# Transposing q and k with DMAs instead of TensorE in the later blocks of a linear-attention and SiLU-MLP kernel

## The chip, the core and the metric

The kernel runs on one core of a Trainium2 chip. The core has five engines that work side by side: TensorE for matrix products (PE in the profile; PEld is its loading of weights), VectorE (DVE), ScalarE (ACT), GpSimd (POOL) and SyncE (SP), which here issues DMAs. Each engine takes its instructions in the order in which the program lists them, and semaphores make one wait for another. Sixteen DMA engines move data between HBM and SBUF, the on-chip memory; PE writes into eight banks of PSUM. The metric is the device time of one execution in microseconds, as the median of several.

## The reference

There are 4 sequences of 768 positions, with 8 heads of 64 elements. Attention is linear with decay: each head h has a factor lam, and

```python
for b in range(nb):
    intra = np.einsum('bhic,bhjc->bhij', qb, kb) * Dmask[None]
    intra = np.einsum('bhij,bhjd->bhid', intra, vb)
    inter = np.einsum('bhid,bhde->bhie', qb * lam_pow[None], kv_state)
    out[:, :, sl] = intra + inter
    kb_dec = kb * rev_pow[None]
    kv_state = lam_block * kv_state + np.einsum('bhsd,bhse->bhde', kb_dec, vb)
```

Dmask is lower triangular with powers of lam. The 3072 rows of 512 that come out go through two dense products with a SiLU between them:

```python
h = x @ w_in                      # 512 -> 2048
g = h * (1.0 / (1.0 + np.exp(-h)))
return g @ w_out                  # 2048 -> 512
```

Inputs and output are float32; the kernel's products take bf16 operands.

## The kernel before

**Attention by blocks.** The 3072 rows are cut into 24 blocks of 128 positions, 6 to a sequence. For a block u the kernel loads k and v (128 positions by 8 heads by 64, float32, 256 KB each) with one DMA each (line 261). q is loaded for two blocks at once (line 264, 512 KB) except for blocks 0, 1, 22 and 23, which are called plain. DVE scales q by powers of lam into bf16 `qs` (line 315) and k into bf16 `ks` (line 369). Scores need q and k with the head's elements on the partitions, so both are transposed. In the kernel before, PE does this with an identity matrix into a PSUM bank: four 128x128 transposes for each block of q (line 327), four for each block of k (line 389). From there ACT or DVE copies q into `qT` (line 336) and k into `kTz` (line 397). In `kTz` each head of a pair of heads stands on its 64 partitions and the other 64 hold zeros, so that a product with the pair's `qT` yields the scores of one head alone. Spreading keys so takes two copies of 64 partitions by 512 elements. For the first 8 blocks (`WIDE = 8`) the zeros are put in before the transpose: `ks` is a padded tile `kp` (line 361), there are eight transposes (line 377) and one copy of 1024 elements, and the state's product is done by head (line 480, eight products of 64 columns) and not by pair of heads (line 484, four of 128), with one sum on DVE (line 500) and not two halves.

Then PE computes scores (line 415), DVE applies the mask and evicts them as `st_sb` (line 424), PE multiplies them with the values `vz` and adds the state's part (lines 453 and 457), and ACT or DVE evicts the result as `xt`. The state is carried from block to block by the sum on line 500 and two multiplications on POOL.

**The dense part.** Attention rows are grouped (first groups of 1 or 2 blocks, later of 4). For a group the first product (line 545) takes 13.8 us of PE when it has 4 blocks; SiLU runs on ACT (line 554); the second product (line 573) runs block by block, then an eviction and a store. The weights are loaded and cast between the first loads of attention.

**The order of the work.** Nothing is emitted in the order of the loops. Every step is handed to a planner (`Plan`, lines 14 to 96) with the engines that may do it and an assumed duration on each, the steps it needs, a priority, and the buffers that it takes and frees (`alloc`, `frees`, named rings with a fixed number of slots). `Plan.run` simulates this greedily and emits all instructions by planned start time. So each engine's order is fixed when the program is written, by assumed durations. Loads form one chain on a resource "SP": 1.19 us for a k, 1.15 for a v, 1.8 for a q of two blocks, 1.36 for a weight piece; they are emitted `AHEAD = 1.8` us before their planned start. A step of resource "NONE" takes no time and can carry a delay: from block 8 on, q, k and v are held to be there only 4.0 us after their load's end (`late`, lines 307 and 355). Stores are a resource "STORE", but are issued from SP too, so loads and stores share one queue in order of planned time. PE idle time before 90 us of the plan may be filled with warm-up products (line 650).

The names that matter below: `kf`, `vf`, `qf` are the rings of loaded blocks (6, 6 and 3 slots), `qs` (2), `qT` (4), `ks` (4), `kTz` (3) those of scaled and transposed blocks, `tr` a PSUM bank for transposes (two at a time).

Of the kernel before, what the change touches and what calls it, by code (L numbers as in the profile page):

```python
# [8 lines left out]
BF16 = mybir.dt.bfloat16  # L9
# [4 lines left out]
class Plan:  # L14
# [3 lines left out]

    AHEAD = 1.8
    AWAY = 0.6  # L20
    LAT = {"SP": 0.0, "NONE": 0.0, "STORE": 2.0, "PE": 0.25, "DVE": 0.12, "ACT": 0.16, "POOL": 0.15, "DMA": 0.1}

    def __init__(self):
        self.ops = []
# [75 lines left out]
def kernel(  # L100
# [10 lines left out]
    nc = tc.nc  # L111
    B, H, S, D = q.shape
    assert (B, H, S, D) == (4, 8, 768, 64)
    BLK = 128
    NB = S // BLK
    NU = B * NB
    NP = H // 2
# [3 lines left out]
    KI = DM // 128  # L121
    KO = DFF // 128
    HB = BLK // 2
    WIDE = 8

    ctx.enter_context(tc.manual_schedule())
    const = ctx.enter_context(tc.tile_pool(name="const", bufs=1))
# [1 line left out]
    ps = ctx.enter_context(tc.tile_pool(name="ps", bufs=1, space=bass.MemoryType.PSUM))  # L129

    plan = Plan()
    BUFS = dict(kf=6, vf=6, qf=3, wst=6, qs=2, qT=4, ks=4, g=34, st_sb=6, o_sb=3, y=2, Xf=2,
                kTz=3, vz=3, Xz=2, kp=3)
    for name, n in BUFS.items():
        plan.ring(name, n)
    plan.ring("bank", 8, pick=True)
# [4 lines left out]
    def sb(o, name, shape, dtype, tag=None):  # L141
        return work.tile(shape, dtype, tag=tag or name, bufs=BUFS[tag or name], name=name)

    def bank(o, name, shape, dtype):
# [5 lines left out]
        out=lam_sb,  # L150
        in_=bass.AP(tensor=lam.tensor, offset=lam.offset, ap=[[0, 128]] + list(lam.ap)),
# [17 lines left out]
        out=ident, in_=ident, compare_op=AL.not_equal, fill=1.0,  # L169
# [6 lines left out]
        out=mask, in_=mask, compare_op=AL.is_ge, fill=0.0,  # L176
        base=0, pattern=[[1, BLK]], channel_multiplier=-1,
    )

    kTz = [const.tile([128, NP, 2, BLK], BF16, name=f"kTz{i}") for i in range(BUFS["kTz"])]  # L180
    vz = [const.tile([128, NP, 4, 64], BF16, name=f"vz{i}") for i in range(BUFS["vz"])]
    Xz = [const.tile([128, NP, 128], BF16, name=f"Xz{i}") for i in range(BUFS["Xz"])]
    kp = [const.tile([128, NP, 2, 128], BF16, name=f"kp{i}") for i in range(BUFS["kp"])]
# [19 lines left out]
    for hh in range(2):  # L203
        r = slice(64 * hh, 64 * hh + 64)
# [15 lines left out]
    val = {}  # L220

    def copy(o, dst, src):
        if o["eng"] == "ACT":
            nc.scalar.activation(dst, src, AF.Copy)  # L224
        else:
            (nc.vector if o["eng"] == "DVE" else nc.gpsimd).tensor_copy(dst, src)  # L226
# [20 lines left out]
    for n, (kind, j) in enumerate(order):  # L247
# [7 lines left out]
        def fn(o, kind=kind, j=j, tag=tag):  # L255
            b, blk = divmod(j, NB)
            sl = slice(blk * BLK, (blk + 1) * BLK)
            if kind in "kvq" and tag != "qf":
                t = sb(o, kind + "f", [128, H, 64], F32, tag)
                src = dict(k=k, v=v, q=q)[kind]  # L260
                nc.sync.dma_start(out=t, in_=src[b, :, sl, :].rearrange("h s d -> s h d"))
            elif kind == "q":
                t = sb(o, "qf", [128, H, 128], F32)
                nc.sync.dma_start(
                    out=t, in_=q[b, :, blk * BLK:(blk + 2) * BLK, :].rearrange("h (p t) d -> p h (t d)", t=2))
            elif kind == "i":
                t = sb(o, "wst", [128, 2, 512], F32)
                m, a = divmod(j, 2)
                nc.sync.dma_start(out=t, in_=w_in_r[:, 2 * a:2 * a + 2, m * 512:(m + 1) * 512])
            else:  # L270
                t = sb(o, "wst", [128, 2, DM], F32)
                nc.sync.dma_start(out=t, in_=w_out_r[:, 2 * j:2 * j + 2, :])
            val[kind + "f", j] = t


        o = plan.op({"SP": us}, [prev], fn, n, alloc=[tag])
# [18 lines left out]
    O = {}  # L295

    def attention(u):
        b, blk = divmod(u, NB)
        pr = at["v", u]


        if u in plain or u % 2 == 0:
            two = u not in plain
            lq = load["q", u]
            late = []
            if u >= 8:
                late = [plan.op({"NONE": 0.0}, [lq], lambda o: None, 0, after=4.0)]
            halves = []
            for t in range(2 if two else 1):
                def fn(o, t=t, first=(t == 0)):  # L310
                    qf = val["qf", u]
                    if first:
                        val["qs", u] = sb(o, "qs", [128, 2, H, 64], BF16)
                    src = qf.rearrange("p h (t d) -> p h t d", t=2)[:, :, t, :] if two else qf
                    nc.vector.tensor_tensor(  # L315
                        val["qs", u][:, t], src,
                        lam_fwd[:, 1 + t if two else 0, :, None].to_broadcast([128, H, 64]), op=AL.mult)
                halves.append(plan.op(
                    {"DVE": 0.7}, [lq] + late + halves[:1], fn, pr + 0.1, alloc=["qs"] if t == 0 else [],
                    frees=[(lq, lq["tag"])] if t == two else []))  # L320
            trs = []
            for t in range(len(halves)):
                def fn(o, t=t):
                    if t == 0:
                        val["trq", u] = bank(o, "tr", [128, len(halves), NP, BLK], BF16)
                    for i in range(NP):
                        nc.tensor.transpose(val["trq", u][:, t, i, :], val["qs", u][:, t, 2 * i:2 * i + 2, :], ident)  # L327
                trs.append(plan.op({"PE": 0.225}, [halves[t]] + trs[:1], fn, pr + 0.1,
                                   alloc=["bank", "n_tr"] if t == 0 else [],
                                   frees=[(halves[0], "qs")] if t == len(halves) - 1 else []))  # L330
            evs = []
            for t in range(len(halves)):
                def fn(o, t=t):
                    if t == 0:
                        val["qT", u] = sb(o, "qT", [128, 2, NP, BLK], BF16)
                    copy(o, val["qT", u][:, t], val["trq", u][:, t])
                evs.append(plan.op({"ACT": 0.6, "DVE": 0.69}, [trs[t]] + evs[:1], fn, pr + 0.1,
                                   alloc=["qT"] if t == 0 else [],
                                   frees=[(trs[0], "bank"), (trs[0], "n_tr")] if t == len(halves) - 1 else []))
            O["qT", u] = evs  # L340
            if two:
                O["qT", u + 1] = evs
        home = u if u in plain else u - u % 2

        def qT(p):
# [5 lines left out]

        lk, lv = load["k", u], load["v", u]
        late = []
        if u >= 8:
            late = [plan.op({"NONE": 0.0}, [lv], lambda o: None, 0, after=4.0)]

        wide = u < WIDE
        if wide:
# [13 lines left out]
        ks = plan.op({"DVE": 0.7}, [lk] + late, fn, pr, alloc=[ring_k], frees=[(lk, lk["tag"])])  # L372
        if wide:
            def fn(o):
                val["trk", u] = bank(o, "tr", [128, 2 * NP, BLK], BF16)
                for i in range(2 * NP):
                    nc.tensor.transpose(val["trk", u][:, i, :], val["ks", u][:, i // 2, i % 2, :], ident)  # L377
            tk = plan.op({"PE": 0.45}, [ks], fn, pr, alloc=["bank", "n_tr"])

            def fn(o):  # L380
                val["kTz", u] = kTz[o["slots"]["kTz"]]
                copy(o, val["kTz", u].rearrange("p a b s -> p (a b) s"), val["trk", u])
            kz = [plan.op({"ACT": 1.02, "DVE": 1.22}, [tk], fn, pr, alloc=["kTz"],
                          frees=[(tk, "bank"), (tk, "n_tr")])]
        else:
            def fn(o):
                val["trk", u] = bank(o, "tr", [128, NP, BLK], BF16)
                for i in range(NP):
                    nc.tensor.transpose(val["trk", u][:, i, :], val["ks", u][:, 2 * i:2 * i + 2, :], ident)  # L389
            tk = plan.op({"PE": 0.225}, [ks], fn, pr, alloc=["bank", "n_tr"])  # L390
            kz = []
            for hh in range(2):
                def fn(o, hh=hh):
                    if hh == 0:
                        val["kTz", u] = kTz[o["slots"]["kTz"]]
                    r = slice(64 * hh, 64 * hh + 64)
                    copy(o, val["kTz", u][r, :, hh, :], val["trk", u][r])
                kz.append(plan.op({"ACT": 0.59, "DVE": 0.69}, [tk] + kz[:1], fn, pr,
                                  alloc=["kTz"] if hh == 0 else [],
                                  frees=[(tk, "bank"), (tk, "n_tr")] if hh else []))  # L400
# [9 lines left out]
        for half in range(2):  # L410
            def fn(o, half=half):
                val["st", u, half] = bank(o, "st", [128, 4, BLK], F32)
                for i in range(4):
# [5 lines left out]
                         alloc=["bank", "n_st"])  # L419

            def fn(o, half=half):
# [6 lines left out]
                                 frees=[(st, "bank"), (st, "n_st")]))  # L428
# [16 lines left out]
        def fn(o):  # L445
# [4 lines left out]
            for p in range(NP):  # L450
# [5 lines left out]
                if blk > 0:  # L456
                    nc.tensor.matmul(x[:, p, :], lhsT=val["Xz", u][:, p, :], rhs=qT(p), start=False, stop=True)  # L457
        oo = plan.op({"PE": 0.0556 * (8 if blk == 0 else 12)}, masks + [vc] + prev_x + ([O["out", u - 1]] if u else []), fn, pr + 0.4,
                     alloc=["bank", "n_x"], frees=gives)
# [14 lines left out]
        def fn(o):  # L474
            d = bank(o, "d", [128, NP, 64 if wide else 128], F32)
            val["d", u] = d
            for p in range(NP):
# [5 lines left out]
                else:  # L483
# [4 lines left out]
                     alloc=["bank", "n_d"], frees=[(ks, ring_k)])  # L488
# [161 lines left out]
                nc.tensor.matmul(t, lhsT=zeros[:, 0:128], rhs=zeros, start=True, stop=True)  # L650
        seq.append((a, len(seq), dict(fn=fn)))

    seq = plan.run({"PE": 1.9, "DVE": 4.2, "ACT": 5.9, "POOL": 5.0, "SP": 3.7, "STORE": 0.0, "NONE": 0.0}, idle)
    for _, _, o in seq:
        o["fn"](o)

# [29 lines left out]
```

## Time and profile before

Three runs took 235.18, 235.65 and 235.69 us, a median of 235.65. The profiled execution is another one:

| | |
|---|---|
| profiled execution, whole | 237.28 us |
| its span, first to last instruction | 235.6 us |
| busy: PE / DVE / ACT / POOL | 221.8 / 114.7 / 121.9 / 53.1 us |
| mean granted TensorE clock | 0.998 |
| moved by DMA | 33.85 MB in 73060 packets, 55376 of them under 512 B |
| landing of a k, v, double q load after issue (median) | 5.5, 5.3, 5.9 us |
| last load issued | 109.34 us |
| last dense product ends | 230.5 us |

How to read the views: a group's row names line, engine, operation, written tile, read tiles, shape and count; then busy time, mean nanoseconds of one, and the idle time of the engine just before, with what ended it. In a timeline the columns are start, length and the instruction, with the wait before it in brackets. The rows of stretches give busy time of each engine within a window. The chain of waits goes back from the last instruction to what released each step. Matmuls are pipelined, so the mean of one is longer than the time from one to the next; the chain shows the latter.

### The profile page before, as it was taken

To read this page: it belongs to the slowest core of one execution; us is meant where nothing else is said; L and a number is where in the kernel's file an instruction comes from. 1 tells how busy PE (TensorE), PEld (TensorE's weight loads), DVE (VectorE), ACT (ScalarE), POOL (GpSimd) and SP (SyncE) were. 2 spreads that over 40 slices of the span, in tenths; PEclk is the share of its full clock that TensorE was granted. 3 is DMA by queue.
4 is the path that set the end of the run, shared out by engine and by line. 5 is a ranking of instruction groups with operands and counts; after the bars stand their busy time and mean duration, and the time that the engine had idled before them with its cause. 6 is when DMAs were issued, how large, how long until landed. Compare 5 with 4: busy or idle time off the path is not lost.

```text
span 235.6 us, 4440 instructions
## 1 busy us (share of the span) xinstructions
PE 221.8 (94%) x1799; PEld 136.3 (58%) x1799; DVE 114.7 (49%) x184; ACT 121.9 (52%) x213; POOL 53.1 (23%) x71
## 2 busy tenths in 40 slices
PE   4889898999999999979999999999999999999994
PEld 1656687899756676746667544444444444444453
DVE  5677755694359999998997211012100111021221
ACT  5585477867777699869976422401275023710000
POOL 7354420340045244642476100000000000000000
PEclk9999999999999999999999999999999999999999
DMA  6999989999999999999200122204400232023232
GB/s 124 237 288 298 294 227 226 296 363 318 221 228 245 255 262 222 233 238 219 46 1 12 35 47 45 45 2 87 92 0 0 45 75 61 0 45 83 56 86 89
DMA packets 73060, 33.85 MB, mean 144 GB/s; under 512 B 55376, under 2 KB 66000, under 8 KB 73040
## 3 DMA queue, kind: packets, MB, share of 16 engines
q1 hardware_dynamic: 72896, 33.50, 60.4%
q8 instruction: 14, 0.23, 0.4%
q10 hardware_dynamic: 144, 0.07, 0.1%
q14 instruction: 6, 0.05, 0.1%
HBM read 27.27 MB, written 6.29 MB: 142 GB/s over the span
## 4 chain that ended last, share of the span: by engine, by line
PE 52%; DVE 2%; DMA 1%; ACT 1%; issue 0%; DVEq 0%
PE o_ps L573 28%; PE h_ps L545 19%; PE x_ps L453 1%; PE st_ps L415 1%; DVE st_sb L424 1%; PE o_ps L612 1%; DMA out_dram<-o_sb 1%; PE x_ps L457 1%; PE d_ps L484 1%; PE tr_ps L327 0%; PE tr_ps L389 0%; DVE ks L369 0%; DVE y L500 0%; ACT kTz L224 0%; DVE o_sb L226 0%
## 5 line engine op out<-in xcount | busy, mean ns | idle before, releaser
L545 PE MATMUL h_ps<-xt,w_in_bf 128*128 128x512 bf16 (+2 forms) x576 | 88.9, 308 | 0.0
L554 ACT ACTIVATE g<-h_ps 128x512 bf16<-128x512 f32 x96 | 56.3, 597 | 59.2 <-PE h_ps L545 33.0
L573 PE MATMUL o_ps<-w_out_bf,g 128*128 128x512 bf16 x368 | 83.3, 379 | 0.5 <-DVE st_sb L424 0.5
L545 PEld LDWEIGHTS <-w_in_bf 128*128 128x128 bf16 x576 | 49.7, 98 | 29.1 <-DVE w_in_bf L226 0.3
L226 DVE COPY o_sb<-o_ps 128x512 f32<-128x512 f32 (+2 forms) x24 | 15.9, 663 | 87.1 <-PE o_ps L573 84.5
L573 PEld LDWEIGHTS <-g 128*128 128x128 bf16 x368 | 35.2, 98 | 39.6 <-issue 0.7
L229 POOL TENSOR_TENSOR Xz<-y,lam_blk 64x256 bf16<-64x256 f32 x40 | 34.3, 858 | 75.0 <-DVE y L500 46.0
L424 DVE TENSOR_TENSOR st_sb<-st_ps,mask 128x512 bf16<-128x512 f32 x48 | 30.9, 683 | 6.0 <-PE st_ps L415 5.7
L224 ACT ACTIVATE kTz<-tr_ps 64x512 bf16<-64x512 bf16 (+1 forms) x38 | 25.8, 680 | 6.6 <-PE tr_ps L377 2.2
L315 DVE TENSOR_TENSOR qs<-qf,lam_fwd 128x512 bf16<-128x512 f32 x24 | 20.2, 861 | 5.0 <-DMA qf<-in_q_dram 5.0
L224 ACT ACTIVATE xt<-x_ps 128x512 bf16<-128x512 f32 x24 | 14.2, 594 | 9.2 <-PE x_ps L457 8.8
L453 PE MATMUL x_ps<-st_sb,vz 128*128 128x128 bf16 x192 | 18.0, 219 | 0.2
L453 PEld LDWEIGHTS <-vz 128*128 128x128 bf16 x192 | 15.1, 98 | 5.4 <-issue 1.2
L500 DVE TENSOR_TENSOR y<-d_ps,Xf 64x256 f32<-64x256 f32 (+1 forms) x27 | 11.3, 419 | 9.9 <-issue 7.6
L415 PE MATMUL st_ps<-qT,kTz 128*128 128x128 bf16 x192 | 15.1, 222 | 0.5 <-ACT qT L224 0.3
L224 ACT ACTIVATE qT<-tr_ps 128x512 bf16<-128x512 bf16 x22 | 12.8, 594 | 4.4 <-PE tr_ps L327 4.3
L229 POOL TENSOR_TENSOR Xf<-y,lam_blk 128x256 f32<-128x256 f32 x16 | 14.5, 909 | 1.3
L457 PE MATMUL x_ps<-qT,Xz 128*128 128x128 bf16 x80 | 14.5, 219 | 0.0
L415 PEld LDWEIGHTS <-kTz 128*128 128x128 bf16 x192 | 12.5, 99 | 3.1 <-ACT kTz L224 1.0
L224 ACT ACTIVATE o_sb<-o_ps 128x512 f32<-128x512 f32 (+1 forms) x2 | 0.9, 438 | 25.6 <-DMA out_dram<-o_sb 25.6
L369 DVE TENSOR_TENSOR ks<-kf,lam_bwd 128x512 bf16<-128x512 f32 x16 | 14.0, 879 | 0.3
L327 PE MATMUL tr_ps<-ident,qs 128*128 128x128 bf16 x96 | 9.1, 223 | 4.0 <-DVE qs L315 3.8
(54 smaller groups left out, 115.8 us busy)
## 6 DMA issues: line engine op xcount, KB each, us to landing
kf<-in_k_dram SPq DMA_DIRECT2D x24, 256.0 KB, 5.5
vf<-in_v_dram SPq DMA_DIRECT2D x24, 256.0 KB, 5.3
out_dram<-o_sb SPq DMA_DIRECT2D x41, 128.0 KB, 2.4
qf<-in_q_dram SPq DMA_DIRECT2D x10, 512.0 KB, 5.9
wst<-in_moe_w_in_dram SPq DMA_DIRECT2D x8, 512.0 KB, 6.9
wst<-in_moe_w_out_dram SPq DMA_DIRECT2D x8, 512.0 KB, 7.3
qf<-in_q_dram SPq DMA_DIRECT2D x4, 256.0 KB, 5.1
out_dram<-o_sb SPq DMA_DIRECT2D x3, 256.0 KB, 3.6
```

The costliest lines, as they stand in the source:

```text
L224: nc.scalar.activation(dst, src, AF.Copy)
L226: (nc.vector if o["eng"] == "DVE" else nc.gpsimd).tensor_copy(dst, src)
L229: (nc.vector if o["eng"] == "DVE" else nc.gpsimd).tensor_tensor(dst, a, b, op=op)
L315: nc.vector.tensor_tensor(val["qs", u][:, t], src, lam_fwd[:, 1 + t if two else 0, :, None].to_broadcast([128, H, 64]), op=AL.mult)
L369: nc.vector.tensor_tensor(val["ks", u], val["kf", u], lam_bwd[:, :, None].to_broadcast([128, H, 64]), op=AL.mult)
L415: nc.tensor.matmul(val["st", u, half][:, i, :], lhsT=val["kTz", u][:, h // 2, h % 2, :], rhs=qT(h // 2), start=True, stop=True)
L424: nc.vector.tensor_tensor(val["st_sb", u, half], val["st", u, half], m[:, None, :].to_broadcast([128, 4, BLK]), op=AL.mult)
L453: nc.tensor.matmul(x[:, p, :], lhsT=vp[:, p, hh, :], rhs=val["st_sb", u, h // 4][:, h % 4, :], start=(hh == 0), stop=(hh == 1 and blk == 0))
L457: nc.tensor.matmul(x[:, p, :], lhsT=val["Xz", u][:, p, :], rhs=qT(p), start=False, stop=True)
L545: nc.tensor.matmul(t[:, j, :], lhsT=w_in_bf[:, ko, (m * per + j) * 128:(m * per + j + 1) * 128], rhs=xts[g][:, ko, :], start=(ko == 0), st ...
L554: nc.scalar.activation(t, val["h", g, m], AF.Silu)
L573: nc.tensor.matmul(val["o", u], lhsT=val["g", g, ko][:, i * BLK:(i + 1) * BLK], rhs=w_out_bf[:, ko, :], start=(ko == 0), stop=(ko == KO - 1))
```

## The change

From block `XB = 8` on, PE transposes neither q nor k. SP issues a transposing DMA from SBUF to SBUF in their place: for q, `qs` goes to `qT` in one DMA for both blocks of a pair (one for a plain block); for k, `ks` goes to a new tile `kT` (ring of 3), from which two copies of 64 partitions spread the keys into `kTz` as before, now reading SBUF, with DVE named first. The planner is given a new resource "XBAR" for these DMAs, one after another, at 2.0 us for 128x512 elements (4.0 for a pair's q), and what needs them is planned 3.0 us after that. They are issued on SP, in the same queue as loads and stores, without the 1.8 us that loads are emitted ahead. The copies and banks of the q transposes disappear for these blocks.

For blocks 4 to 7 the loads of q, k and v are now counted 1.2 us late. Padded keys are used for four blocks in place of eight, so blocks 4 to 7 go by the narrow path, still with transposes on PE. The `qf` ring has 2 slots in place of 3.

```diff
-    LAT = {"SP": 0.0, "NONE": 0.0, "STORE": 2.0, ...
+    LAT = {"SP": 0.0, "XBAR": 0.0, "NONE": 0.0, "STORE": 2.0, ...
...
-    WIDE = 8
+    XB = 8
+    WIDE = 4
...
-    BUFS = dict(kf=6, vf=6, qf=3, wst=6, qs=2, qT=4, ks=4, g=34, st_sb=6, o_sb=3, y=2, Xf=2,
-                kTz=3, vz=3, Xz=2, kp=3)
+    BUFS = dict(kf=6, vf=6, qf=2, wst=6, qs=2, qT=4, ks=4, g=34, st_sb=6, o_sb=3, y=2, Xf=2,
+                kTz=3, vz=3, Xz=2, kp=3, kT=3)
...
-            if u >= 8:
-                late = [plan.op({"NONE": 0.0}, [lq], lambda o: None, 0, after=4.0)]
+            if u >= 4:
+                late = [plan.op({"NONE": 0.0}, [lq], lambda o: None, 0, after=4.0 if u >= 8 else 1.2)]
...
+            if u >= XB:
+                n = len(halves)
+
+                def fn(o):
+                    val["qT", u] = sb(o, "qT", [128, 2, NP, BLK], BF16)
+                    nc.sync.dma_start_transpose(
+                        out=val["qT", u][:, 0:n].rearrange("p t a s -> p (t a) s"),
+                        in_=val["qs", u][:, 0:n].rearrange("p t h d -> p (t h d)"))
+                x = plan.op({"XBAR": 2.0 * n}, [halves[-1]], fn, pr + 0.1, alloc=["qT"], frees=[(halves[0], "qs")])
+                O["qT", u] = [x, plan.op({"NONE": 0.0}, [x], lambda o: None, 0, after=3.0)]
-            for t in range(len(halves)):
+            for t in range(len(halves) if u < XB else 0):
...
-        if u >= 8:
-            late = [plan.op({"NONE": 0.0}, [lv], lambda o: None, 0, after=4.0)]
+        if u >= 4:
+            late = [plan.op({"NONE": 0.0}, [lv], lambda o: None, 0, after=4.0 if u >= 8 else 1.2)]
...
+        elif u >= XB:
+            def fn(o):
+                val["kT", u] = sb(o, "kT", [128, NP, BLK], BF16)
+                nc.sync.dma_start_transpose(
+                    out=val["kT", u], in_=val["ks", u].rearrange("p h d -> p (h d)"))
+            tk = plan.op({"XBAR": 2.0}, [ks], fn, pr, alloc=["kT"])
+            landed = plan.op({"NONE": 0.0}, [tk], lambda o: None, 0, after=3.0)
+            kz = []
+            for hh in range(2):
+                def fn(o, hh=hh):
+                    if hh == 0:
+                        val["kTz", u] = kTz[o["slots"]["kTz"]]
+                    r = slice(64 * hh, 64 * hh + 64)
+                    copy(o, val["kTz", u][r, :, hh, :], val["kT", u][r])
+                kz.append(plan.op({"DVE": 0.35, "ACT": 0.59}, [tk, landed] + kz[:1], fn, pr,
+                                  alloc=["kTz"] if hh == 0 else [], frees=[(tk, "kT")] if hh else []))
...
-    seq = plan.run({"PE": 1.9, ..., "SP": 3.7, "STORE": 0.0, "NONE": 0.0}, idle)
+    seq = plan.run({"PE": 1.9, ..., "SP": 3.7, "STORE": 0.0, "NONE": 0.0, "XBAR": 0.0}, idle)
```

## The prediction

> **What bounds the kernel now.** I read the share of busy time first, then the busy time by stage, because an average hides that three resources take turns.
>
> ```profile
> PE 221.8 (94%) x1799; PEld 136.3 (58%) x1799; DVE 114.7 (49%) x184; ACT 121.9 (52%) x213; POOL 53.1 (23%) x71
> PEclk9999999999999999999999999999999999999999
> ```
> ```profile
> 70.00:80.00 10.00, 9.70 (x98) 6.33 (x96) 9.78 (x17) 7.22 (x13) 5.15 (x6) 1.00 1.03 259
> 80.00:90.00 10.00, 10.00 (x114) 7.16 (x112) 9.76 (x17) 8.96 (x17) 3.01 (x4) 1.00 1.11 241
> 90.00:100.00 10.00, 10.00 (x107) 6.93 (x106) 9.78 (x16) 9.00 (x17) 5.96 (x7) 1.00 0.98 235
> 100.00:110.00 10.00, 8.61 (x85) 5.64 (x84) 9.87 (x16) 7.84 (x15) 4.14 (x5) 1.00 1.27 232
> 110.00:120.00 10.00, 10.00 (x104) 6.89 (x103) 9.04 (x15) 9.32 (x19) 4.88 (x6) 1.00 0.39 68
> ```
> The columns after the length are PE, PEld, DVE, ACT and POOL busy time, the granted clock, the DMA share and GB/s. From 70 to 110 us PE is full, DVE is full (39.2 of 40 us), and the DMA engines are full. After 115 us nothing is loaded any more, and from 120.7 us on the chain of waits is PE alone, from 133.8 us dense products only, to 230.5 us. The clock never falls. So PE work taken out anywhere after about 50 us shortens the span, if PE isn't made to wait: its order is fixed when the program is written, and an operand that comes later than the planner thought stops everything behind it. It hardly happens now. The waits from 60 us on are 0.30, 1.39 and 0.46 us.
>
> ```profile
> 103.45 0.40 PE L484 MATMUL d_ps<-vz,ks 128*128 128x128 bf16 x4 [1.39 <-DVE vz L226]
> 120.73 1.02 PE L573 MATMUL o_ps<-w_out_bf,g 128*128 128x512 bf16 x4 [0.46 <-DVE st_sb L424]
> ```
> The third view is the load queue, SP's timeline.
>
> ```profile
> 59.80 1.13 SPq L264 DMA_DIRECT2D qf<-in_q_dram  x1
> ...
> 103.34 1.09 SPq L261 DMA_DIRECT2D qf<-in_q_dram  x1
> 104.53 1.04 SPq L261 DMA_DIRECT2D kf<-in_k_dram  x1
> 105.66 1.23 SPq L261 DMA_DIRECT2D vf<-in_v_dram  x1
> 106.94 1.14 SPq L261 DMA_DIRECT2D qf<-in_q_dram  x1
> 108.13 1.11 SPq L261 DMA_DIRECT2D kf<-in_k_dram  x1
> 109.34 1.09 SPq L261 DMA_DIRECT2D vf<-in_v_dram  x1
> ```
> The reader is to see that SP issues load after load without a pause, each held about 1.1 us by the full queue (an issue into an emptier one took 0.42 us). Six pairs of blocks lie between the two q rows: 43.54 / 6 = 7.26 us a pair. The planner counts 1.80 + 2 x 1.19 + 2 x 1.15 = 6.48 us a pair, so the loads slip 0.78 us a pair, some 5 us over the stage, and PE paid 2.15 us of it in waits, a share of 0.43. The rest went into the 4 us by which blocks from 8 on are counted late.
>
> **The sum's base.** Span 235.6 us; the profiled execution took 237.28 us in all, so 1.7 us lie around the span. The median of the runs shown, 235.65, is 1.6 us under that execution. I add the terms to the span and read the result as a median: both are 235.6.
>
> **PE: transposes leave.** Two rows carry it (groups by form).
>
> ```profile
> L389 PE MATMUL tr_ps<-ident,ks 128*128 128x128 bf16 x64 | 6.0, 219 | 0.0
> L327 PE MATMUL tr_ps<-ident,qs 128*128 128x128 bf16 x64 | 5.7, 219 | 0.4 <-DVE qs L315 0.3
> ```
> They are of the stretch from 60 to 135 us: count, busy us, mean ns of one, idle before. The 64 on line 327 are 7 pairs at 8 and 2 single blocks at 4, so this is exactly what blocks 8 to 23 need, and all 128 go. The mean of 219 ns overlaps with its neighbours; in the chain of waits four take 0.22 us and eight 0.45, 55.6 ns each: 128 x 0.0556 = 7.1 us. All lie in the stage where PE is the limit: **-7.1 us**, hidden by nothing.
>
> **Blocks 4 to 7.** Unpadded keys halve 32 transposes (16 x 0.0556 = 0.9 us) and turn 24 products of line 480 (1.2 us) into 12 of 0.0556 (0.7 us): 1.4 us of PE. Counting the loads 1.2 us late moves dense work in front of operations that PE waited for at 40.71 (1.00 us) and 47.39 (0.75 us). At best -3.2; at worst the three more halved sums on DVE (3 x 0.42 us) come onto the path, +1.3. Work saved before 50 us partly becomes waiting: I take the middle of the better half, **-1.5**.
>
> **ACT and DVE.** ACT loses 30 key copies (17.6 us) and 15 query copies (8.6 us). DVE gains 32 copies of 64x512; the nearest row, the same shape from PSUM, took 0.413 us, so 13.2 us less the three PSUM copies it loses (1.2): 12 us on an engine that has 0.8 us free between 70 and 110. The cover is ACT: it has 26 us less, and casts of values, evictions of outputs and of attention results can go there. Value **0**; without that cover up to +6 (half of 12, the other half lying in 110 to 130, where DVE has 3 us free in 20); below nothing -2, the ACT relief answering the 1.39 and 0.46 us waits.
>
> **SP and the DMA engines.** 16 transposing DMAs for k, 7 for q pairs, 2 for the q of the last blocks: 25 issues, 32 units of 128x512 bf16 (131 kB). All stand in SP's queue, between the loads, and share its rings. No row shows one. Lower end by bytes: 131 kB at the best slice of the page, 363 GB/s: 0.36 us. Upper end: the 2.0 us a unit that the planner is given for them; a store of the same size, 128 KB, took 2.4 us from issue to landing, alone. I take a price by packets: a k load is 1024 packets of 256 B at 1.1 us, a unit of bf16 rows cut into 128 columns has 512 of the same size, so 0.55 us. How many get in front of the last load? The planner runs them one after another at 2.0 us from the first keys (60.1 us, first line 369) to the last load (109.3): at most 24; the q pairs wait for their second half, so 21. The last load then issues 21 x 0.55 = 11.5 us later, at about 121 us.
>
> [...]
>
> What part of 11.5 us reaches PE? Between the measured share of 0.43 (4.9 us) and all of it. I take all: the 4 us of lateness are used up by today's slip, and the transposing DMA itself stands in SP's order behind the slipping loads, then has scores (line 415) on PE and masks on DVE queued behind it. **+11.5**. The qf ring of two costs nothing: the q load at 89.45 needs the buffer that the scaling at 83.52 frees, 4.6 us earlier; without that, its wait would be a load's 1.1 us.
>
> **New waits.** SP now waits for the scaled block (line 369 or 315) before it issues a transposing DMA, with later loads and stores behind it. Today's loads land 5.3 to 5.9 us after issue; the planner allows 2.0 + 3.0. **+0.5**; at the ends 0, and 1 us at each of 17 issues before the last load, +17.
>
> **Sum**: -7.1 - 1.5 + 0 + 11.5 + 0.5 = +3.4, so 239.0 us (profiled execution about 240.7).
>
> **Rivals.** *Slip absorbed, faster.* Speaking for it: 5 us of slip cost PE 2.15. At 0.36 us a unit, 7.6 x 0.43 = 3.3: -8.6 + 3.3 + 0.5 gives 230.8; with nothing charged, 227.0. Against: no margin is left in the load queue. It decides below a delay of 8.1 us, which is 0.39 us a unit if all of it is paid. Chance 0.37.
> *Transposing DMAs much dearer, or SP held at each wait, slower by far.* 1.0 us a unit gives 21 us, 248.5; 2.0 gives 42, 269.5; SP waits of 1 us add 17, 255.5. For it: full rings, in-order SP. Against: loads in flight keep the rings fed for about 5 us while SP waits. Chance 0.17.
> *Change not felt*: the two sides cancel within 0.2% (0.5 us), about what a measurement of this kernel can tell from no change. Chance 0.04.
> *Forecast*, 236.2 to 247: 0.42.
>
> **Numbers.** Slower 0.42 + 0.17 = 0.59, faster 0.37, same 0.04. The range goes from 229 (under it the case with next to nothing charged, 0.09) to 254 (above it 0.11). The likeliest case alone spans 236.2 to 247.
>
> **What will show it.** No tr_ps groups after block 8, and about 1.4 us less of them and of line 480 before; the last load issued near 121 us (109 or less speaks for the first rival, 130 or more for the second); PE waits between 70 and 130 us of about 12 us, released by kTz, qT or st_sb; landing of the transposing DMAs at 5 to 6 us. The prediction is wrong if the DMA share has room that the page doesn't show, if the planner's 2.0 us a unit spreads attention so that slipping loads meet no waiting PE, or if DVE's copies, not SP, hold the scores.

## The result and the profile after

The changed kernel takes 242.91 us (median of four, 241.59 to 244.82) against 235.48 us: a ratio of 1.031, with a 95% interval of 1.025 to 1.037. It is slower by 7.4 us. The forecast was 3.4 us, the right sign and less than half of the size. Of all the kernels here only e3 has runs more than 1.5% above its fastest; its median and ratio are those of the five runs below that.

The stages between 70 and 130 us, with the columns as before (PE, PEld, DVE, ACT, POOL busy time, clock, DMA share, GB/s):

```profile
70.00:80.00 10.00, 7.16 (x46) 3.62 (x45) 4.91 (x10) 2.30 (x4) 1.52 (x3) 0.83 1.22 249
80.00:90.00 10.00, 7.94 (x66) 4.64 (x65) 6.56 (x13) 3.69 (x8) 4.87 (x6) 1.00 1.34 216
90.00:100.00 10.00, 7.16 (x62) 4.31 (x60) 5.19 (x9) 2.81 (x7) 1.88 (x3) 1.00 1.14 218
100.00:110.00 10.00, 8.42 (x58) 4.32 (x57) 8.43 (x15) 5.72 (x12) 5.35 (x6) 1.00 0.85 189
110.00:120.00 10.00, 9.03 (x79) 5.35 (x77) 8.67 (x16) 6.03 (x11) 2.17 (x3) 1.00 1.20 218
120.00:130.00 10.00, 6.70 (x47) 3.71 (x45) 6.42 (x15) 4.13 (x8) 3.61 (x5) 0.83 1.37 194
```

PE, full before, is busy 46.4 of 60 us. DVE and ACT now have room (40.2 and 24.7 of 60 us): over the whole span ACT lost 18 us of work (121.9 to 103.6) and DVE gained 2 (114.7 to 116.8), and both wait. Only the DMA engines are still full, with a share of 0.85 to 1.37. PE's own timeline names what it waited for:

```profile
74.33 1.02 PE L443 MATMUL st_ps<-qT,kTz 128*128 128x128 bf16 x8 [2.75 <-DVE kTz L227]
86.06 0.89 PE L443 MATMUL st_ps<-qT,kTz 128*128 128x128 bf16 x8 [1.97 <-DVE kTz L227]
93.88 0.27 PE L481 MATMUL x_ps<-st_sb,vz 128*128 128x128 bf16 x2 [1.06 <-DVE st_sb L452]
96.65 0.61 PE L443 MATMUL st_ps<-qT,kTz 128*128 128x128 bf16 x8 [1.68 <-DMA qT<-qs]
101.63 0.89 PE L443 MATMUL st_ps<-qT,kTz 128*128 128x128 bf16 x8 [1.33 <-DVE kTz L227]
118.88 0.28 PE L481 MATMUL x_ps<-st_sb,vz 128*128 128x128 bf16 x2 [0.89 <-DVE st_sb L452]
126.46 1.25 PE L443 MATMUL st_ps<-qT,kTz 128*128 128x128 bf16 x8 [3.19 <-DVE kTz L227]
```

The brackets add up to 12.9 us, where the kernel before had 2.15. Five of them, 10.9 us, wait for a transposed block (`kTz` or `qT`), the other two, 1.95 us, for masked scores (`st_sb`). DVE was not late with its copies; it waited itself, for the transposing DMA (rows of the waits from 60 to 135 us: total, times, longest):

```profile
DVE kTz L227 <- DMA kT<-ks: 15.9, 6, 4.2
...
PE st_ps L443 <- DVE kTz L227: 9.2, 4, 3.2
...
ACT kTz L225 <- DMA kT<-ks: 6.3, 3, 4.3
```

SP's timeline shows where the DMAs stand:

```profile
120.31 1.78 SPq L400 DMA_TRANSPOSE kT<-ks  x1
122.15 0.57 SPq L262 DMA_DIRECT2D qf<-in_q_dram  x1
122.83 2.73 SPq L400 DMA_TRANSPOSE kT<-ks  x1
125.61 0.57 SPq L262 DMA_DIRECT2D kf<-in_k_dram  x1
126.23 0.57 SPq L262 DMA_DIRECT2D vf<-in_v_dram  x1
126.91 2.20 SPq L328 DMA_TRANSPOSE qT<-qs  x1
...
130.47 0.90 SPq L262 DMA_DIRECT2D vf<-in_v_dram  x1
```

Most loads now take 0.43 to 0.58 us of SP, not 1.1, and a transposing DMA takes 1.2 to 3.2 us. The last load issues at 130.5 us and not at 109.3. From the q load at 59.31 us to this one, SP spent 32.4 us on 17 transposing DMAs, 25.7 on loads and 7.0 on stores, and paused for 6.1 us.

Who waits for whom can be read from DVE's timeline, which shows when two of these blocks were scaled, a q and a k:

```profile
102.83 0.92 DVE L316 TENSOR_TENSOR qs<-qf,lam_fwd 128x512 bf16<-128x512 f32 x1
110.28 0.68 DVE L381 TENSOR_TENSOR ks<-kf,lam_bwd 128x512 bf16<-128x512 f32 x1
```

The first is the only one for which SP stood waiting before the last load: SP was free at 102.64 and issued the transposing DMA at 103.82, a wait of 1.1 us. The second was ready at 110.95 and was issued at 120.31, because loads, stores and other transposing DMAs stood before it in SP's order. In the 17 transposing DMAs ahead of the last load, matched in order with DVE's scaling, a block lay ready for 7.9 us in the median before its DMA was issued. Over all 25 it was 6.4 us to the issue and 10.5 to the landing, where the planner counts 5.0 from scaled to usable for a k. So the transposed blocks were late because they stood behind the other DMAs, and hardly because SP waited for them.

And in the two stages with a clock of 0.83, the clock was halved for 3.41 us each time (0.50 in the rows of 75 to 78 and 127 to 129 us), around the end of the two longest waits (2.75 and 3.19 us): a second bill of up to 1.7 us for each, estimated as half of 3.41.

### The profile page after: what moved, and what is told of

It is laid out like the page before. It is cut to its first block, busy times and chain, and to the rows that moved or that the text cites. A ratio compares the mean times of both kernels' runs of the same rounds, so it can differ in the third digit from the quotient of the medians.

```text
span 241.7 us, 4186 instructions
## 1 busy us (share of the span) xinstructions
PE 219.8 (91%) x1645; PEld 130.1 (54%) x1645; DVE 116.8 (48%) x205; ACT 103.6 (43%) x183; POOL 50.8 (21%) x71
## 3 DMA queue, kind: packets, MB, share of 16 engines
q1 hardware_dynamic: 90080, 37.70, 73.5%
## 4 chain that ended last, share of the span: by engine, by line
PE 64%; DMA 18%; SPq 8%; DVE 6%; issue 2%; ACT 1%; DVEq 0%
PE o_ps L601 28%; PE h_ps L573 28%; DMA kT<-ks 11%; SPq L262 5%; DMA wst<-in_moe_w_in_dram 4%; PE st_ps L443 3%; PE x_ps L481 2%; DMA qT<-qs 2%; DVE qs L316 2%; DVE kTz L227 1%; DVE st_sb L452 1%; PE x_ps L485 1%; SPq L270 1%; PE o_ps L640 1%; DVE y L528 1%
## 5 line engine op out<-in xcount | busy, mean ns | idle before, releaser
L573 PE MATMUL h_ps<-xt,w_in_bf 128*128 128x512 bf16 (+2 forms) x576 | 89.9, 310 | 0.3 <-ACT xt L225 0.3
L230 POOL TENSOR_TENSOR Xz<-y,lam_blk 64x256 bf16<-64x256 f32 x40 | 32.8, 820 | 97.6 <-DVE y L528 56.1
L443 PE MATMUL st_ps<-qT,kTz 128*128 128x128 bf16 x192 | 16.7, 228 | 11.8 <-DVE kTz L227 9.2
L316 DVE TENSOR_TENSOR qs<-qf,lam_fwd 128x512 bf16<-128x512 f32 x24 | 18.2, 774 | 4.6 <-DMA qf<-in_q_dram 4.5
L225 ACT ACTIVATE vz<-vf 128x512 bf16<-128x512 f32 x21 | 13.2, 627 | 9.7 <-DMA vf<-in_v_dram 9.6
L227 DVE COPY kTz<-kT 64x512 bf16<-64x512 bf16 x26 | 8.6, 331 | 17.5 <-DMA kT<-ks 17.0
L528 DVE TENSOR_TENSOR y<-d_ps,Xf 64x256 f32<-64x256 f32 (+1 forms) x29 | 12.2, 421 | 6.5 <-issue 2.3
L381 DVE TENSOR_TENSOR ks<-kf,lam_bwd 128x512 bf16<-128x512 f32 x20 | 14.8, 750 | 0.5 <-DMA kf<-in_k_dram 0.2
L230 POOL TENSOR_TENSOR Xf<-y,lam_blk 128x256 f32<-128x256 f32 x16 | 13.7, 856 | 1.3
L678 PE MATMUL warm_ps<-zeros 128*128 128x512 bf16 x29 | 9.5, 448 | 1.3 <-DVE pos L162 1.3
```

Source lines behind the costliest of these rows:

```text
L230: (nc.vector if o["eng"] == "DVE" else nc.gpsimd).tensor_tensor(dst, a, b, op=op)
L316: nc.vector.tensor_tensor(val["qs", u][:, t], src, lam_fwd[:, 1 + t if two else 0, :, None].to_broadcast([128, H, 64]), op=AL.mult)
L381: nc.vector.tensor_tensor(val["ks", u], val["kf", u], lam_bwd[:, :, None].to_broadcast([128, H, 64]), op=AL.mult)
L443: nc.tensor.matmul(val["st", u, half][:, i, :], lhsT=val["kTz", u][:, h // 2, h % 2, :], rhs=qT(h // 2), start=True, stop=True)
L573: nc.tensor.matmul(t[:, j, :], lhsT=w_in_bf[:, ko, (m * per + j) * 128:(m * per + j + 1) * 128], rhs=xts[g][:, ko, :], start=(ko == 0), st ...
```

## The experiments

Three explanations had to be told apart. *Packets*: the DMA engines have 16384 more packets of 256 B to move, so everything comes late. *SP held*: loads stand behind SP's waits for scaled blocks and behind the issue of transposing DMAs. *Order*: being late costs nothing by itself; it costs because the order of PE, and of SP, is fixed by a planner that doesn't know of it. All medians below are against the kernel before on the same chip (235.3 to 235.5 us).

### The part on blocks 4 to 7 alone (e1, e8)

```diff
-    XB = 8
+    XB = 24
```

> The changed kernel with every transpose back on TensorE (XB = 24): what is left of the change is the part on blocks 4 to 7 (four padded blocks, loads counted 1.2 us late) and the qf ring of two. The prediction's term: -1.5 us, about 234.0. The trace of the changed kernel has PE busy 2.9 us more between 20 and 50 us than before, so up to -3 (232.5) if all of that is kept. Rival: work done sooner only turns into waiting later, 235.5, no change.

Measured: 232.67 us, ratio 0.988 (0.985 to 0.991). So this part is worth 2.9 us and not 1.5. It also is the right base for the rest: moving the transposes cost 10.2 us, from 232.67 to 242.91. To split it, eight padded blocks were put back:

```diff
-    WIDE = 4
+    WIDE = 8
```

> e1 with eight padded blocks, as before (WIDE = 8): what is left is the 1.2 us of lateness for blocks 4 to 7 and the qf ring of two. It splits e1's -2.9 us. If the waits at 40.71 and 47.39 us (1.75 us) are the gain, 233.5 to 234.2, and the 1.4 us of PE work are the rest; if the work is the whole gain, 235.5.

Measured: 235.32 us, ratio 0.999 (0.997 to 1.002). Counting the loads late and the smaller qf ring together bring nothing by themselves, though the waits at 40.71 and 47.39 us are gone from the trace. The gain comes with the unpadded keys, 2.7 us, more than the 1.4 us of PE work they remove. What the rest is wasn't separated (the unpadded keys without the late count were not run).

### The same DMAs with nothing gained (e4)

```diff
+            if u >= 8:
+                def fn(o, n=len(halves)):
+                    t = sb(o, "dq", [128, 2, NP, BLK], BF16)
+                    nc.sync.dma_start_transpose(
+                        out=t[:, 0:n].rearrange("p t a s -> p (t a) s"), in_=w_out_bf[:, 0:n, :].rearrange("p t d -> p (t d)"))
+                plan.op({"XBAR": 2.0 * len(halves)}, [halves[-1]], fn, pr + 0.1)
...
+        if u >= 8:
+            def fn(o):
+                t = sb(o, "dk", [128, NP, BLK], BF16)
+                nc.sync.dma_start_transpose(out=t, in_=w_out_bf[:, 2, :])
+            plan.op({"XBAR": 2.0}, [ks], fn, pr)
```

> e1 with 25 transposing DMAs added at the places that the planner gives them, all of which read a weight tile that has long been ready and write tiles that nobody reads; q and k still go over TensorE. It has their packets and their issue on SP, but no wait for a scaled block, no round trip before the scores, and no PE work saved. Theory 'packets': 23 units of 0.6 us before the last load, which issues near 123 us (109 in the kernel before), and 6 to 12 us over e1. Theory 'waits' (SP waiting for scaled blocks and the trip of 4 to 6 us to the scores are what costs): last load under 118 us, less than 4 us over e1.

Measured: 249.21 us, 16.5 over e1, ratio 1.059 (1.056 to 1.062). The last load issues at 124.74 us (SP's timeline):

```profile
122.24 1.78 SPq L394 DMA_TRANSPOSE dk<-w_out_bf  x1
124.06 0.58 SPq L262 DMA_DIRECT2D kf<-in_k_dram  x1
124.74 0.53 SPq L262 DMA_DIRECT2D vf<-in_v_dram  x1
```

In e1 it is 111.27:

```profile
111.27 1.08 SPq L262 DMA_DIRECT2D vf<-in_v_dram  x1
```

So 21 units ahead of it (five pairs of q, eleven k) delay it by 13.5 us, 0.64 us each, without any wait for a scaled block. This price holds both the packets and SP's own time for the issue; e4 by itself doesn't tell one from the other. But the 16 transposing DMAs held SP for 32.1 us, 12.9 more than 16 times the 1.20 us that is the least one takes, so SP was held by more than the least time of an issue. That a full queue held it is the author's estimate; no run shows how full it was.

In the two profiled executions PE is idle 22.9 us against 13.1, 9.8 more, and the clock was halved twice for 3.41 us, which is up to 3.4 us of work: 13.2 together, of a difference in span of 13.5 (247.1 against 233.6). So in this pair the delay of 13.5 us cost PE as much, about three quarters of it as waiting. The other 3 us between the medians come from the profiled executions: e1's took 235.33 us, 2.7 above its median, e4's 248.84, 0.4 under; what they are stays open. "Waits" falls as the main cause; "packets" named the last load rightly, and the time is above its 6 to 12 us.

Comparing this with the changed kernel, which does the same DMAs and drops the transposes on PE, gives 242.91 - 249.21 = -6.3 us. If the 7.1 us of PE work was saved in full, 0.8 us is the balance of all else in which the two differ: the trip to the scores, the later loads, the copies.

The last load of the change issues 5.7 us later than here. By SP's rows from the same q load on, four more stores stand before it (+3.5 us for stores), one more transposing DMA for a pair of q (+0.3 for all of them), and SP pauses 2.0 us more, of which 1.1 is the one wait for a scaled block.

### Another queue (e3)

```diff
-                    nc.sync.dma_start_transpose(
+                    nc.scalar.dma_start_transpose(
```

> The changed kernel with its 25 transposing DMAs issued from ACT, not from SP: the same packets on the same engines, but SP's loads stand behind none of their waits and issues. Theory 'SP held' (the loads wait for SP while it waits for scaled blocks and for the 1.2 us and more of each issue): last load at 118 us or sooner, in place of 130.5, and 233 to 238. Theory 'packets' (16384 more packets of 256 B fill the DMA engines): last load still at 125 to 130, and 240 or more. ACT is busy 27 of 70 us between 60 and 130, so 25 issues of 1.2 us, 30 us, should fit.

The edit stands in both places, for q and for k. Measured: 236.46 us, ratio 1.005 (1.001 to 1.008), last load at 124.15 us (SP's timeline):

```profile
122.38 1.68 SPq L262 DMA_DIRECT2D kf<-in_k_dram  x1
124.15 1.48 SPq L262 DMA_DIRECT2D vf<-in_v_dram  x1
```

Each expectation is half right: the time is where "SP held" had it, the last load nearly where "packets" had it. Without the transposing DMAs on it SP issues the last load 6.3 us earlier than in the change, and the kernel is 6.4 us faster. But 12.9 us of delay against e1 remain, though SP issues no transposing DMA: a load now holds it for 1.3 us in the mean (45.8 us for 35 loads; 42.6 in e1, 25.7 in the change). So the greater part of the delay doesn't lie in SP's issues. It isn't all packets either: ten stores stand before the last load and not six, and SP pauses 7.1 us and not 3.3. The medians can't say more than that: the ten runs spread from 235.1 to 240.3.

### The same lateness, known to the planner (e2, e7, e6)

```diff
+        if kind in "kvq" and j >= 8:
+            us *= 1.6
```

This stands where the planner is given the length of a load: 10.4 us for a pair of blocks and not 6.48. The trace of the changed kernel has q loads at 59.31 and 122.15 us, six pairs apart, 10.5 us a pair.

> The changed kernel, with the planner told that loads from block 8 on take 1.6 times as long (10.4 us a pair, as its trace shows), nothing else. Theory 'order': the price is not that operands come late but that PE's fixed order doesn't know it; then PE waits from 60 us on fall from 12.9 us to under 5, and the time to about 231 to 234. Theory 'queue': attention itself has become too slow for PE, whatever the order; then PE still lacks work for 8 us or more and the time stays at 239 to 243.

Measured: 228.73 us, ratio 0.972 (0.968 to 0.977). PE's waits from 60 us on fall from 12.9 to 4.2 us, and the time is better than either expectation. The last load of this kernel issues even later, at 139.70 us (SP's timeline), and the kernel is 14.2 us faster than the change:

```profile
137.72 0.58 SPq L264 DMA_DIRECT2D kf<-in_k_dram  x1
138.40 1.21 SPq L330 DMA_TRANSPOSE qT<-qs  x1
139.70 0.53 SPq L264 DMA_DIRECT2D vf<-in_v_dram  x1
```

PE has dense work of earlier blocks in hand. If the order puts it in front of late scores, lateness costs little; if the order doesn't, PE stands still beside it. SP's order changed as well: a scaled block now lies ready for 0.8 us in the median, over all 25, before its transposing DMA is issued (6.4 in the change). The useless DMAs of e4 have no such part, because nobody waits for them. The same edit on them:

> e4 (25 useless transposing DMAs on SP, all real transposes on TensorE) with loads from block 8 on planned 1.6 times as long. Theory 'order': the same 16384 packets cost PE nothing once the order allows for them: 232 to 236, against 249.2 in e4. Theory 'packets': 243 or more.

Measured: 233.02 us, ratio 0.992 (0.989 to 0.995), against 249.21 with the old order. The last load is at 135.9 us. And the control, e1 with the pace that its loads had:

```diff
+        if kind in "kvq" and j >= 8:
+            us *= 1.12
```

> Control for the slow plan: e1 (all transposes on TensorE) with loads from block 8 on planned 1.12 times as long, the 7.26 us a pair that the kernel before shows. Theory 'order': e1's PE waits from 60 us on (3.9 us) shrink by 1 to 3 us, 230 to 232. If it came to 228.7, the slow plan's gain would have nothing to do with the DMAs; if it stays at 232.7, waits of this size are not the plan's fault.

Measured: 231.20 us, ratio 0.983 (0.981 to 0.985); its timeline shows no PE wait from 60 us on. So 1.5 us of the gain have nothing to do with the DMAs, and against this base 25 useless DMAs cost 1.8 us (233.02), where the old order made them cost 16.5. This decides for *order*. The base has the factor 1.12 and e7 1.6; e1 with 1.6 was not run, so how much of the 1.8 is the factor's isn't known.

### What the change is worth with the right order (e5, e9 to e12)

First e2 with the DMAs issued from ACT:

> The changed kernel with both: transposing DMAs issued from ACT, and loads from block 8 on planned 1.6 times as long. If the order was all that the DMAs cost, 227 to 230, like the slow plan alone (228.7). If the issue on ACT (25 times 1.2 us in front of SiLU and evictions) is a price of its own, 231 to 235, with PE waits released by ACT.

Measured: 228.53 us, ratio 0.972 (0.968 to 0.975). Issue on ACT is no clear price and no clear gain in this order.

Only half of the blocks (`XB = 16`, the factor 1.12 for blocks 8 to 15 and 1.6 from 16 on), on SP and on ACT:

> Only blocks 16 to 23 go through transposing DMAs (on SP), loads planned 1.12 times as long for blocks 8 to 15 and 1.6 times from 16 on. Half of the transposes leave TensorE: 16 groups of 0.2225 us, 3.6 us. If the order covers the DMAs, e6 less 3.6: 227.6, and better than the whole change with the right order (228.7), because attention is held up for half as long. If the short of work between 80 and 120 us that e2 shows only moves to a later stage, 229 to 231.

> The same as e9 with the DMAs issued from ACT. Within 1 us of e9 if SP's waits are covered by the order as well, as e2 and e5 suggest.

Measured: 228.11 us, ratio 0.969 (0.967 to 0.972), and 228.79, ratio 0.972 (0.969 to 0.975). Half of the transposes off PE gain 3.1 us over e6, of 3.6. From all blocks e2 and e5 had only 2.5 and 2.7, of 7.1: there the order still had something wrong. Two guesses at what, the first on e2, the second on e5:

```diff
-            us *= 1.6
+            us *= 1.9
```

> e2 with loads planned 1.9 times as long, not 1.6. The last load of e2 issues at 139.7 us, so its order is near what the loads can do. If 1.6 was still too fast, PE's 4.2 us of waits shrink and it comes to 226 to 228; if 1.6 was enough, attention starves PE by plan and it is 229 to 233.

Measured: 228.87 us, ratio 0.973 (0.970 to 0.976). No difference to 1.6; a slower pace was not what was missing.

```diff
-            landed = plan.op({"NONE": 0.0}, [tk], lambda o: None, 0, after=3.0)
+            landed = plan.op({"NONE": 0.0}, [tk], lambda o: None, 0, after=5.0)
```

The same for q, with the DMAs on ACT and loads 1.6 times as long.

> e5 (ACT, loads planned 1.6 times as long) with what needs a transposed tile planned 5.0 us after the DMA and not 3.0. e5's PE waits from 60 us on are 2.7 us, 1.66 of them one wait for xt. If the DMAs' trip is what the order still gets wrong, 226.5 to 228; if not, 228 to 230.

Measured: 226.02 us, ratio 0.961 (0.958 to 0.964): 9.2 us under the kernel before, the best version found, and a little better than expected. In e5 a block took 5.3 us in the median and 7.6 at most from scaled to landed; the planner had allowed 2.0 + 3.0 us for a k, and now allows 7.0. PE's waits from 60 us on fell from 2.7 to 1.25 us, the one for xt from 1.66 to 0.46. That is 1.5 of the 2.5 us gained; where the rest lies wasn't shown. Its stages:

```profile
80.00:100.00 20.00, 18.95 (x147) 10.77 (x146) 16.86 (x29) 7.90 (x16) 7.09 (x9) 1.00 1.22 243
100.00:120.00 20.00, 19.91 (x166) 11.89 (x167) 16.35 (x31) 14.08 (x26) 6.82 (x8) 1.00 1.32 220
120.00:140.00 20.00, 19.74 (x145) 11.09 (x144) 15.05 (x28) 12.72 (x24) 7.29 (x9) 1.00 1.04 172
```

PE is busy 58.6 of these 60 us, with loads that end at 127 us, 18 us later than before. From e6 to this kernel, moving the transposes to DMAs brings 5.2 of the 7.1 us of PE work.

## Why the prediction was right or wrong

The terms against what the runs showed, by medians (the last column names the pair):

| term | predicted | measured | by |
|---|---|---|---|
| blocks 4 to 7, late count, qf ring | -1.5 | -2.9 | before to e1 |
| transposing DMAs in the queue, paid by PE | +11.5 | +16.5 | e1 to e4 |
| transposes leave PE, and new waits | -7.1 + 0.5 = -6.6 | -6.3 | e4 to the change |
| DVE copies | 0 | in the line above | |
| sum | +3.4 | +7.3 (result +7.4) | |

The count of the PE term was right: from e1 to the change PE has 128 weight loads fewer (1773 and 1645), one for each transpose. Its 7.1 us fit the -6.3 here, and at best 5.2 of them were seen as a gain (e6 to e11); no run shows them alone. The zero for DVE was right: the copies took 0.29 us in the median and not 0.41, six of 32 went to ACT, and DVE's whole work rose by 2 us, not 12.

The price of a unit was nearly right: 0.55 us by the count of packets, 0.64 measured, with 21 units ahead of the last load in e4 as counted (23 in the change). The trace has exactly 512 packets of 256 B for a unit: 16384 more than before.

The step that failed is the term of +11.5, "What part of 11.5 us reaches PE?", answered by "all", as waiting alone. It measured 16.5 by the medians and 13.5 in the profiled pair of e1 and e4. The delay behind it was mis-sized by 2 us: 13.5 and not 11.5 (0.09 us a unit). In the pair PE paid 9.8 us of it as waiting, and up to 3.4 us came from the halved clock, which the prediction put at nothing. It had read "The clock never falls" from the kernel before, where no wait was longer than 1.4 us in this stage, and never asked what 2 to 3 us of standing still would do to it. The change shows the same two halvings. The 3 us between the pair and the medians stay open. The waiting was forecast well: "about 12 us" of PE waits between 70 and 130 us, and 12.9 measured.

"New waits, +0.5" is near the balance of 0.8, but that is luck, because the direction was wrong. SP hardly waits for scaled blocks, 1.1 us before the last load; scaled blocks wait for SP, 7.9 us in the median. The prediction had this where it says that the transposing DMA "stands in SP's order behind the slipping loads", but gave it no time of its own. The last load at 130.5 us is past its mark of 130 for the dearer rival, and yet that rival's 248.5 us did not come: a late last load is no measure of the price. Landing took 4.2 to 4.5 us in the median and not 5 to 6.

Blocks 4 to 7: the halving of the gain ("partly becomes waiting") was wrong, and so was the reason given for the other half. The waits at 40.71 and 47.39 us were removed without any gain (e8).

The first rival, that the slip is absorbed, was ruled out for this order and true for another. What the prediction named as a way to be wrong, "if the planner's 2.0 us a unit spreads attention so that slipping loads meet no waiting PE", needed more than the 2.0 us (e2): the planner gave the DMAs a resource of their own and left the loads at their old pace, while both go through one queue (q1 takes 72896 packets before and 90080 in the change) and are issued from SP.

In bytes, 131 kB for 0.64 us of delay between loads is 205 GB/s, near the 238 GB/s of a k load (262 kB in 1.1 us). After the last load of the change, an issue of two units held SP for 1.25 us and issues of one unit for 1.21 to 1.27 us, so SP's time there goes by the issue and not by the bytes. No run here shows what transposing DMAs reach by themselves.

## What to carry to other kernels

In a kernel whose order is written out ahead, a transfer is priced by what the order knows of it: the same 25 DMAs cost 16.5 us in one order and 1.8 in another, with later loads in the second. When work moves from an engine to the DMA queues, give the planner the new pace of everything that shares the queue, and more than the bare trip for what needs the moved data (here 5.0 us behind the DMA's own 2.0, not 3.0), before judging the move. Look also at how long a ready operand lies before its transfer is issued: here it was longer than the transfer. Judge it against a base that has only the rest of the change: here a gain of 2.9 us hid in front of a loss of 10.2.

## What the runs showed of the hardware

The granted clock was halved for 3.41 us around the end of PE waits of 2.75 and 3.19 us (change: it fell at 74.94 and 126.14 us, the waits ended at 74.33 and 126.46), and in e4 after waits of 2.60 and 1.75 us (a mean of 0.62 from 95 to 99 us and of 0.60 from 105.5 to 109). Waits of 1.97 us in the change, 2.23 in e4 and 2.58 in e3 were not followed by it (1.00 from 86 to 88, 86 to 90 and 126 to 134 us), so the length of the wait alone doesn't decide. Where it falls seems to matter: the first five clock records of the change begin 64.85, 3.41, 47.79 and 3.41 us apart, which are 19, 1, 14 and 1 steps of 3.413 us, and the two falls of e4, placed by its rows at about 95.95 and 106.2 us, are three such steps apart. Counted back from the falls, the steps at whose end the clock fell held 2.84, 2.92, 2.60 and 1.85 us of idle PE. One step of e4 with 1.95 us was not followed by a fall, so no sharp limit is shown. Each time costs up to 1.7 us, estimated as half of 3.41.

```profile
73.00:79.00 6.00, 4.58 (x26) 2.34 (x27) 4.11 (x9) 1.26 (x2) 0.00 (x0) 0.72 1.20 228
125.50:130.00 4.50, 3.51 (x15) 1.76 (x16) 3.76 (x9) 0.55 (x1) 0.42 (x1) 0.62 1.28 222
```

These are two stretches of the changed kernel; the clock is the third number from the end, 0.72 and 0.62 in the mean where PE had waited.

A transposing DMA from SBUF to SBUF held SP for at least 1.20 us where it moved 131 kB (change) and at least 1.23 where it moved 262 (e4), where most loads' issues beside them took 0.43 to 0.58 us; and it landed 4.2 to 4.5 us after issue in the median of the change, 2.4 at the least (in e3, issued from ACT, 5.9 to 6.4 us in the median).
